# Weight blocks converted in pairs, one product with the reciprocal sums, and TensorE's fixed order from step 12, in a one-core attention and feed-forward kernel

## The chip, the cores and the metric

The kernel runs on one core of a Trainium2 chip. The metric is the device time of one execution in microseconds (us), as the median of several runs. A core has TensorE (PE, matmuls and transposes), VectorE (DVE), ScalarE (ACT), GpSimd (POOL) and SyncE (SP, which issues most transfers); each works through its own list of instructions in order, and semaphores make one wait for another.

## The reference

Attention with sink tokens and a sliding window, then a feed-forward block on its output:

```python
q, k, v: [4, 8, 768, 64] float32;  n_sink, window = 4, 128
w_in: [512, 2048], w_out: [2048, 512]   (float64)
scores = (q @ k.T) / 8
keep = (pos < n_sink) | ((0 <= rel) & (rel < window))
scores = where(keep, scores, -1e9); a = exp(scores - max)
a = a / (sum(a) + 1e-9);  x = (a @ v) as [3072, 512]
h = x @ w_in;  sp = max(h, 0) + log1p(exp(-|h|))
out = (h * erf(sp)) @ w_out
```

## The kernel before

The 3072 tokens form 12 groups of 256. Attention is cut into 48 steps, four head pairs for each group; step s is group s // 4. A step has these parts, written by one letter each in the order tables: q, v (loads), p (transposes of q and k into tile tqk, copied by ACT to kq), s (score matmuls into ps), f (`soft`: predicated copies and masking with the negative maximum on DVE, then four exponentials with their sums on ACT), n (`norm`: reciprocal of the sums and multiplication of the probabilities pst by it), t (transposes of pst into tile tp, copied by ACT to pt, masked by POOL into uo), w and u (the sink part: sh, ts, sp), a (value matmuls into av, two steps later), x (output of the step as the feed-forward's input, split into a high part xh and a low part xl). From step 9 on (NW) norm multiplies the sink columns apart (sh) and the four 128 x 128 parts of pst by four operations; before, the four parts are 128 x 144. In steps 4 to 7 the four are done on ACT.

Between the steps runs the feed-forward block, in 16 blocks of 128 hidden units per group: H m (hidden matmuls; two blocks share one tile h in one of two buffers), A m (the activation, seven operations on ACT and some on DVE, named r, u, acc, gf and g, with a product of three factors; its result g is split by POOL into two parts), P m (matmuls with w_out into tile o) and R (results). Group 0 works with the weights as single fp32 values (wf, gf, whole products of one matmul each), the others with weights split into a high part (h, `whigh`, a cast on ACT: wt from wf) and a low part (l, `wlow`, a subtraction on DVE), three matmuls for one.

The weights arrive as 64-bit words in 32 blocks of 512 KB (L j, `wload`, tile ws) and are turned into fp32 bits on DVE by three operations on 128 x 512 words each (C j, `wconv`, into half of a tile wf). `wconv` is a generator: one of its operations is put in after each operation of A or of norm (`fill`), and D drains what is left. All block tiles come from one pool of 33 buffers.

The order on each engine: the first steps follow three hand-written lists (LOADS for transfers, VEC for DVE, TEN for TensorE), where an item is placed once what it needs (`needs`) is placed. After these, every part has a key, `pos(s)` being the place of step s, and a scheduler takes ready instructions by priority. An engine's order is held to the keys only while `vec.on` or `ten.on` is set: DVE up to key 50, TensorE in the hand-written part and again from `pos(NF1) - 0.5` on (NF1 = 15). From step NI = 16 on, `together` does values, scores and transposes of a step as interleaved 64-row halves of the array, and q, k and pst of the neighbouring steps are flipped into one tile rt. The helper at L241 (`Line.run`) issues nearly every instruction of DVE and TensorE, so most rows of the trace carry its line.

Of the kernel before, what the change touches and what calls it, by code (L numbers as in the profile page):

```python
# [9 lines left out]
F32 = mybir.dt.float32  # L10
BF16 = mybir.dt.bfloat16
F32R = mybir.dt.float32r
I32 = mybir.dt.int32
AF = mybir.ActivationFunctionType
ALU = mybir.AluOpType
# [4 lines left out]
P = 128  # L20
# [14 lines left out]
LEAD, LAG = 16, 4  # L35

CEND = 50.0
WQ = 5
HI = 6.0
LO = 4.5  # L40

NE, AL = 4, 2
NW = 9
NF1 = 15
NI = 16

PW, EA = 256, 40
O = dict(prep=-100, norm=-100, core=-300, av=-300, load=-400, ptrans=-200, xfin=-100,
# [5 lines left out]
    "L18 L19 L20 L21 L22 q9 v9 L23 L24 L25 L26 L27 L28 L29 L30 L31"  # L54
)
VEC = (
# [3 lines left out]
)  # L60
TEN = (
    "p0 s0 p1 s1 p2 t0 u0 s2 t1 u1 p3 a0 x0 s3 a1 x1 t2 u2 p4 s4 a2 x2 t3 u3 p5 s5 a3 x3 t4 u4 H0 H1 H2 H3 p6 t5 u5 a4 s6 "
# [7 lines left out]
def kernel(  # L70
# [11 lines left out]
    nc = tc.nc  # L82
    B, H, S, D = q.shape
    NT, DM = out.shape
    DF = w_in.shape[1]
    NPAIR = H // 2
    NC = DM // P
# [6 lines left out]
    KB = P + SW  # L94
    scale = 1.0 / math.sqrt(D)

    cpool = ctx.enter_context(tc.tile_pool(name="const", bufs=1))
    wpool = ctx.enter_context(tc.tile_pool(name="wpool", bufs=33))


    ident = cpool.tile([P, P], F32, name="ident")
# [10 lines left out]
    wf = tiny[:, 4:8].rearrange("p (a b) -> p a b", a=2)  # L112
# [23 lines left out]
    wf, wt = {}, {}  # L136

    def fast_path():
        with ExitStack() as st:
# [4 lines left out]
            ps_o = st.enter_context(tc.tile_pool(name="ps_o", bufs=2, space=PSUM))  # L144
            ps_h = st.enter_context(tc.tile_pool(name="ps_h", bufs=2, space=PSUM))
            ps_s = st.enter_context(tc.tile_pool(name="ps_s", bufs=1, space=PSUM))
            first = ExitStack()
            ps_t = first.enter_context(tc.tile_pool(name="ps_t", bufs=2, space=PSUM))
            ps_r = []
# [10 lines left out]
                out=kw[:, :256], in0=rf[:, :256], scalar=0.0, in1=kw[:, :256], op0=ALU.is_ge, op1=ALU.mult  # L160
# [31 lines left out]
            pst = pers.tile([P, RING, 2, 2, KB], F32, name="pst")  # L192
# [55 lines left out]
            vec, ten, syn, sca = (Line(x) for x in (nc.vector, nc.tensor, nc.sync, nc.scalar))  # L248
# [10 lines left out]
            def prep(s):  # L259

                g, c = divmod(s, NPAIR)
                d = stp[s]
                if s <= NI:
                    tp = ps_t.tile([P, 4, P], F32, tag="t", name=f"tqk_{s}")
# [14 lines left out]
            def sinks(s):  # L279
# [14 lines left out]
            def score(s):  # L294
# [32 lines left out]

                if s >= NI:
                    together(s, half)
# [106 lines left out]
            def both(s):  # L436
                return shs[s % 2].rearrange("p r t -> p (r t)")[:, :P].bitcast(F32)

            def norm(s):
                d = stp[s]  # L440
                sm = d["sum"]
                vec.tensor_scalar_add(sm, sm, 1.0e-9)
                fill()
                vec.reciprocal(sm, sm)
                fill()
                if s >= NW:
                    x, y = (
                        t.rearrange("p (o n) t -> p o n t", o=1).broadcast_to([P, 2, 4, SW])
                        for t in (
                            d["pst"].rearrange("p i h t -> p (i h) t")[:, :, P:],  # L450
                            sm.rearrange("p i (h o) -> p (i h) o", o=1).broadcast_to([P, 4, SW]),
                        )
                    )
                    vec.tensor_tensor(both(s).rearrange("p (r n t) -> p r n t", r=2, n=4), x, y, op=ALU.mult)
                for i in range(2):
                    for h in range(2):
                        p = d["pst"][:, i, h, : P if s >= NW else KB]
                        if 4 <= s < 8:
                            nc.scalar.activation(p, p, AF.Copy, scale=sm[:, i, h : h + 1])
                        else:  # L460
                            vec.tensor_scalar_mul(p, p, sm[:, i, h : h + 1])

            def ptrans(s):

# [117 lines left out]
            staged, pair = {}, {}  # L582
            def wload(n):

                src = wblock(n)
                t = staged[n] = wpool.tile([P, 2 * DM], I32, tag="wo", name=f"ws_{n}")
                if src.dtype == F32:
                    syn.dma_start(t[:, :DM].bitcast(F32), src)
                else:
                    syn.dma_start(t, src.bitcast(I32))  # L590

            def wconv(n, wn):

                s = staged.pop(n)
                if wn // 2 not in pair:
                    pair[wn // 2] = wpool.tile([P, 2, DM], F32, tag="wo", name=f"wf_{wn // 2}")
                t = wf[n] = pair[wn // 2][:, wn % 2, :]
                if wblock(n).dtype == F32:
                    nc.scalar.copy(t, s[:, :512].bitcast(F32))
                    return  # L600
                w = s.rearrange("p (n t) -> p n t", t=2)
                ti = t.bitcast(I32)
                vec.tensor_scalar(ti, w[:, :, 1], 0x07FFFFFF, 3, op0=ALU.bitwise_and, op1=ALU.logical_shift_left)
                yield
                vec.scalar_tensor_tensor(
                    out=ti, in0=w[:, :, 1], scalar=-0x40000000, in1=ti, op0=ALU.bitwise_and, op1=ALU.bitwise_or
                )
                yield
                vec.scalar_tensor_tensor(
                    out=ti, in0=w[:, :, 0], scalar=29, in1=ti, op0=ALU.logical_shift_right, op1=ALU.bitwise_or  # L610
                )

            todo = []
# [12 lines left out]

            def whigh(n):

                d = wt[n] = wpool.tile([P, 2, DM], F32R, tag="wo", name=f"wt_{n}")
                nc.scalar.copy(d[:, 0, :], wf[n])  # L630

            def wlow(n):
# [4 lines left out]
            def wblock(n):  # L637
                if n < 16:
                    j, c = divmod(n, NC)
                    return w_in[c * P : (c + 1) * P, WB * j : WB * j + WB]  # L640
                return w_out[(n - 16) * P : (n - 15) * P, :]
# [29 lines left out]
            def use(n):  # L671
# [3 lines left out]
            order = sorted(range(32), key=use)  # L675
# [1 line left out]
                "q": ("load", loadqk), "v": ("load", loadv), "p": ("prep", prep), "k": ("prep", sinks), "s": ("core", score),  # L677
                "f": ("core", soft), "n": ("norm", norm), "t": ("ptrans", ptrans), "w": ("ptrans", sinkw), "u": ("ptrans", strans),
                "a": ("av", av), "x": ("xfin", xfin), "H": ("hid", hid), "A": ("act", act), "P": ("proj", proj), "R": ("res", res),
                "L": ("wl", lambda j: wload(order[j])), "C": ("wc", lambda j: todo.append(wconv(order[j], j))), "D": ("wc", drain),  # L680
                "h": ("ws", whigh), "l": ("ws", wlow),
            }

# [2 lines left out]

            def needs(nm, j):

                pin = [("C", order.index(n)) for n in range(j // NC * NC, j // NC * NC + NC)] if nm == "H" else []
                return {  # L690
                    "p": [("q", j), ("f", j - NPAIR)],
                    "s": [("p", j), ("f", j - 1 if j != 3 else 0)] if j > 1 else [("p", j)],
                    "f": [("s", j), ("t", j - (4 if j < 6 else 2)), ("w", j - (4 if j < 6 else 2))],
                    "n": [("f", j)],
                    "t": [("n", j), ("a", j - AL)],
                    "w": [("n", j), ("u", j - 2)] if j < NW else [("u", j)],
                    "u": [("w" if j < NW else "n", j), ("t", j)],
                    "k": [("v", j), ("p", j)],
                    "a": [("u", j), ("w", j), ("v", j)] + [("k", j)] * (j < NE),
                    "x": [("a", j)],  # L700
                    "H": pin + [("x", 3), ("f", 2), ("H", j - 1)] + [("A", j - 3)] * (j % 2 == 0),
                    "A": [("H", j), ("P", j - 4)],
                    "P": [("A", j | 1), ("C", order.index(16 + j if j < 16 else 0)), ("u", 5)],
                    "q": [("p", j - 2)],
                    "v": [("a", j - 3)],
                    "C": [("L", j)],
                    "L": [("C", j - WQ)],
                }.get(nm, [])

            lines = [words(x) for x in (LOADS, VEC, TEN)]  # L710
# [2 lines left out]
            while any(lines):  # L713
                before = len(done)
                for x in lines:
                    while x and all(w in done for w in needs(*x[0]) if w in known):
                        w = x.pop(0)
# [5 lines left out]

            fixed = pos(NF1) - 0.5
            for s in range(NE, NSTEP + AL):
                a = pos(s)
                if s < NF1:
                    plan = (
# [4 lines left out]
                else:  # L733
# [249 lines left out]
```

## Time and profile before

| | |
|---|---|
| median of 3 runs | 731.14 us (731.11 to 731.46) |
| profiled execution | 730.77 us, of which the span of the instructions is 729.1 us |
| TensorE busy | 695.0 us, 95% of the span |
| DVE busy | 517.6 us, 71% |
| ACT busy | 540.8 us, 74% |
| POOL busy | 193.4 us, 27% |
| mean granted TensorE clock | 0.994 of full speed |

The share of busy time is a mean over stages. A time line row gives the start, the busy time of a group of like instructions that follow each other, the engine, the line, the operation with its tiles (out<-in), and in brackets how long the engine stood idle before it and what it waited for. TensorE's matmuls overlap, so a group's busy time contains the tail of its last matmul, in which the next group already begins.

### The profile page before, as it was taken

The page shows a single profiled execution, that of the slowest core. Times are in us where ns is not written, and L with a number is a line of the kernel's source. Part 1 is how long each engine was busy: PE and PEld are TensorE (multiplying, and loading weights), DVE is VectorE, ACT ScalarE, POOL GpSimd, SP SyncE. Part 2 cuts the span into 40 slices and gives each one's busy share as a digit, 9 for nine tenths or more (in the row PEclk, how much of TensorE's full clock was granted, in tenths as well). Part 3 has the DMA queues.
Part 4 walks back from the last instruction along what each step waited for, and adds up shares of the span by engine and source line. Part 5 has one row for each costly group of instructions (what it writes and reads, how often), then busy time and mean ns, then how long its engine had stood idle before and what let it go on. Part 6 is the DMA issues. An engine that isn't in the chain of part 4 may idle for free. (4 is left out here: it accounts for less than half of the span.)

```text
span 729.1 us, 16134 instructions
## 1 busy us (share of the span) xinstructions
PE 695.0 (95%) x5721; PEld 588.3 (81%) x5721; DVE 517.6 (71%) x1493; ACT 540.8 (74%) x1288; POOL 193.4 (27%) x256
## 2 busy tenths in 40 slices
PE   4798999989999999999999999999999999999996
PEld 2474566777888888988888988988888988988995
DVE  7899998999786666666767667666767667663442
ACT  3576669778788778778878778778878778776663
POOL 2221010333232233234223223234223223232221
PEclk9999999999999999999999999999999999999999
DMA  5778641211212211112212212112212211100000
GB/s 142 213 208 307 212 142 27 63 27 37 60 36 53 59 38 44 55 29 47 58 37 52 59 34 49 55 27 46 59 34 57 58 31 38 41 1 1 30 1 33
DMA packets 100600, 47.40 MB, mean 65 GB/s; under 512 B 89248, under 2 KB 93344, under 8 KB 100512
## 3 DMA queue, kind: packets, MB, share of 16 engines
q1 hardware_dynamic: 99680, 46.16, 22.9%
q8 instruction: 47, 0.77, 0.4%
q14 instruction: 41, 0.34, 0.2%
q10 hardware_dynamic: 832, 0.13, 0.1%
HBM read 37.88 MB, written 6.29 MB: 61 GB/s over the span
## 5 line engine op out<-in xcount | busy, mean ns | idle before, releaser
L241 PE MATMUL o<-wt,g 128*128 128x512 f32 x1056 | 258.1, 393 | 1.1 <-POOLq L951 0.7
L241 PEld LDWEIGHTS o<-wt,g 128*128 128x128 f32 x1056 | 191.7, 188 | 39.3 <-POOLq L951 1.1
L810 POOL TENSOR_TENSOR g<-acc,g 128x512 fp32r<-128x512 f32 x88 | 116.8, 1327 | 382.5 <-DVE g L241 378.9
L241 PE MATMUL h<-xh,wt 128*128 128x256 f32 x1408 | 194.6, 281 | 2.2 <-DVE acc L241 2.1
L241 PEld LDWEIGHTS h<-xh,wt 128*128 128x128 f32 x1408 | 180.0, 189 | 9.0 <-DVE acc L241 3.2
L801 ACT ACTIVATE u<-r 128x512 f32<-128x512 f32 x288 | 162.1, 625 | 5.3 <-DVE gf L241 1.6
L241 DVE SCALAR_TENSOR_TENSOR acc<-u,h 128x512 f32<-128x512 f32 x88 | 60.5, 687 | 135.9 <-PE o L241 79.3
L241 DVE SCALAR_TENSOR_TENSOR acc<-u,acc 128x512 f32<-128x512 f32 x176 | 122.2, 694 | 18.0 <-ACT u L801 0.6
L241 PE MATMUL h<-xl,wt 128*128 128x256 f32 x704 | 110.0, 277 | 0.0
L796 ACT ACTIVATE r<-h 128x512 f32<-128x512 f32 x96 | 57.3, 596 | 68.4 <-PE h L241 68.3
L241 ACT ACTIVATE pst<-pst,kq 128x144 f32<-128x144 f32 x192 | 78.5, 421 | 22.7 <-DVE kq L241 22.4
L241 PEld LDWEIGHTS h<-xl,wt 128*128 128x128 f32 x704 | 93.4, 188 | 0.3 <-DVE wf L241 0.2
L487 POOL TENSOR_SCALAR_AFFINE_SELECT uo<-pt 128x512 f32<-128x512 f32 (+1 forms) x96 | 60.1, 649 | 89.9 <-ACT pt L241 89.8
L241 PE MATMUL ps<-kq 64*64 64x208 f32 (+1 forms) x768 | 70.3, 368 | 7.3 <-ACT kq L241 7.3
L241 PE MATMUL av<-uo,v 64*64 64x192 f32 (+4 forms) x856 | 70.0, 294 | 0.0
L797 ACT ACTIVATE r<-r 128x512 f32<-128x512 f32 x96 | 60.9, 635 | 2.7
L798 ACT ACTIVATE r<-r 128x512 f32<-128x512 f32 x96 | 60.9, 634 | 2.8
L241 PEld LDWEIGHTS ps<-kq 64*64 64x64 f32 x768 | 41.5, 138 | 20.7 <-issue 9.7
L241 PEld LDWEIGHTS av<-uo,v 64*64 64x64 f32 (+1 forms) x856 | 47.7, 134 | 10.3 <-issue 1.9
L241 ACT COPY kq<-rt 128x512 f32<-128x512 f32 (+1 forms) x39 | 19.1, 511 | 46.0 <-PE rt L241 46.0
L241 DVE CUSTOM_DVE_ANT_0 pst<-ps,mask 128x144 f32<-128x144 f32 x192 | 47.6, 304 | 1.6
L241 DVE CAST g<-acc 128x512 fp32r<-128x512 f32 x88 | 38.2, 434 | 8.4
(98 smaller groups left out, 713.7 us busy)
## 6 DMA issues: line engine op xcount, KB each, us to landing
ws<-in_moe_w_in_dram SPq DMA_DIRECT2D x16, 512.0 KB, 5.0
ws<-in_moe_w_out_dram SPq DMA_DIRECT2D x16, 512.0 KB, 7.7
v<-in_v_dram SPq DMA_DIRECT2D x64, 96.0 KB, 2.3
out_dram<-ot SPq DMA_DIRECT2D x24, 256.0 KB, 2.2
q<-in_q_dram SPq DMA_DIRECT2D x95, 64.0 KB, 2.4
k<-in_k_dram SPq DMA_DIRECT2D x95, 64.0 KB, 2.3
v<-in_v_dram SPq DMA_DIRECT2D x32, 64.0 KB, 2.3
kq<-kq SPq DMA_DIRECT2D x32, 64.0 KB, 1.8
```

Of the source, the lines that this page charges most:

```text
L241: ins = f(*a, **k)
L487: nc.gpsimd.affine_select(out=uo[:, :, i1:, e, :], in_=pt[:, :, i1:, :], pattern=[[0, 2], [0, 2 - i1], [-sg, P]], compare_op=op, fill=0.0, ...
L796: nc.scalar.activation(r, h, AF.Tanh, bias=b_t, scale=0.5)
L797: nc.scalar.activation(r, r, AF.Square, bias=b_v, scale=-0.5)
L798: nc.scalar.activation(r, r, AF.Square, bias=b_r)
L801: nc.scalar.activation(u, r, AF.Square, bias=b_a[i], scale=CS)
L810: nc.gpsimd.tensor_tensor(gl, acc, gh.bitcast(F32), op=ALU.subtract)
```

## The change

Conversion: blocks 0 to 3 are converted singly as before, the other 28 in 14 pairs, three DVE operations over 128 x 1024 words each. The raw words lie in a pool of their own (`wraw`, three tiles of two blocks), the other blocks' pool has 27 buffers in place of 33, and a load waits for the conversion that used its tile before. Where the raw pool lay, a pool `wlate` of six buffers opens once it is closed; the split weights with places 20 to 25 in the order of use (blocks 12 to 15 of w_in, 24 and 25 in the count over both matrices) go there. The list VEC names a pair by its even member. Norm: outside steps 4 to 7 the four products of pst become one TENSOR_TENSOR with the reciprocal sums broadcast. Order: NF1 is 12 and NI is 13, so TensorE is held to the keys from step 12 on and works in halves from step 13 on; keys of t, u and P that depend on them change too.

```diff
-WQ = 5
+SOLO = 4
...
-NF1 = 15
-NI = 16
+NF1 = 12
+NI = 13
...
-    "D f6 x4 C12 A3 n6 C13 D w6 C14 C15 A5 C16 C17 D f7 x5 C18 C20 A7 n7 C19 C21 D w7 C22 C23 A9 C24 C25 D f8 x6 C26 A11 n8 "
-    "C27 D w8 C28 C29 A13 x7 C30 C31 D f9 A15"
+    "D f6 x4 C12 A3 n6 D w6 C14 A5 C16 D f7 x5 C18 A7 n7 C20 D w7 C22 A9 C24 D f8 x6 C26 A11 n8 "
+    "D w8 C28 A13 x7 C30 D f9 A15"
...
-    wpool = ctx.enter_context(tc.tile_pool(name="wpool", bufs=33))
+    wpool = ctx.enter_context(tc.tile_pool(name="wpool", bufs=27))
...
+            early = ExitStack()
+            wraw = [early.enter_context(tc.tile_pool(name="wraw", bufs=3, side="right"))]
+            late = []
...
-                for i in range(2):
-                    for h in range(2):
-                        p = d["pst"][:, i, h, : P if s >= NW else KB]
-                        if 4 <= s < 8:
+                n = P if s >= NW else KB
+                if 4 <= s < 8:
+                    for i in range(2):
+                        for h in range(2):
+                            p = d["pst"][:, i, h, :n]
                             nc.scalar.activation(p, p, AF.Copy, scale=sm[:, i, h : h + 1])
-                        else:
-                            vec.tensor_scalar_mul(p, p, sm[:, i, h : h + 1])
+                    return
+                p = d["pst"].rearrange("p i h t -> p (i h) t")[:, :, :n]
+                x = sm.rearrange("p i (h o) -> p (i h) o", o=1).broadcast_to([P, 4, n])
+                vec.tensor_tensor(p, p, x, op=ALU.mult)
...
-                t = staged[n] = wpool.tile([P, 2 * DM], I32, tag="wo", name=f"ws_{n}")
+                j = order.index(n)
+                if j // 2 not in staged:
+                    staged[j // 2] = wraw[0].tile([P, 2, 2 * DM], I32, tag="w", name=f"ws_{j // 2}")
+                t = staged[j // 2][:, j % 2, :]
...
+                n = 1 if j < SOLO else 2
+                s = staged[j // 2][:, j % 2 : j % 2 + n, :]
...
+                t = pair[j // 2][:, j % 2 : j % 2 + n, :]
...
-                d = wt[n] = wpool.tile([P, 2, DM], F32R, tag="wo", name=f"wt_{n}")
+                if 20 <= order.index(n) < 26:
+                    if not late:
+                        early.close()
+                        late.append(st.enter_context(tc.tile_pool(name="wlate", bufs=6, side="right")))
+                    d = wt[n] = late[0].tile([P, 2, DM], F32R, tag="wo", name=f"wt_{n}")
+                else:
+                    d = wt[n] = wpool.tile([P, 2, DM], F32R, tag="wo", name=f"wt_{n}")
...
-                    "C": [("L", j)],
-                    "L": [("C", j - WQ)],
+                    "C": [("L", j if j < SOLO else j + 1)],
+                    "L": [("C", z) for z in (whole(j - j % 2 - 6), whole(j - j % 2 - 5)) if z[1] >= 0],
```

TensorE's own instructions around step 12, before: h_28 are the last hidden matmuls ahead of it, o are the matmuls with w_out (wt_24 and wt_25 are its blocks), tp_12 and ts_12 the transposes of step 12, h_30 the next hidden matmuls.

```order
L241 MATMUL h_28_1859<-xl_1_723,wt_15_1550 128x256
L241 MATMUL o_1_0_1484<-wt_24_1552,g_25_1735 128x512
...
L241 MATMUL o_1_1_1485<-wt_25_1612,g_25_1735 128x512
L241 MATMUL tp_12_1875<-ident_61,pst_138 128x128
L241 MATMUL ts_12_1884<-ident_61,sh0_139 128x128
L241 MATMUL tp_12_1875<-ident_61,pst_138 128x128 x3
L241 MATMUL h_30_1936<-xh_1_722,wt_12_1544 128x256 x2
```

The same place in the change (its helper is at L246), with av_11 and ps_13 as the first values and scores in halves, rt_13 the first joint tile of flips.

```order
L246 MATMUL h_28_1791<-xl_1_711,wt_15_1488 128x256
L246 MATMUL tp_12_1822<-ident_61,pst_145 128x128 x4
L246 MATMUL ts_12_1831<-ident_61,sh0_146 128x128
L246 MATMUL o_1_0_1418<-wt_24_1490,g_25_1670 128x512
...
L246 MATMUL o_1_1_1419<-wt_25_1544,g_25_1670 128x512
L246 MATMUL av_11_1869<-sp_11_1618,sv_143 128x256
...
L246 MATMUL rt_13_1896<-ident_61,q_14_1711 128x64 x4
L246 MATMUL h_30_1926<-xh_1_710,wt_12_1482 128x256 x2
```

The transposes of step 12 have moved from behind the twelve o matmuls to ahead of them, and values, scores and flips of step 13 from behind h_30 to ahead of it.

ACT's instructions ahead of the exponentials of step 9 (pst_138 with its four parts), before: wt are the casts of `whigh`, kq_134 is the copy of step 10's transposes, r and u belong to the activations.

```order
L801 ACTIVATE u2_15_1244<-r_15_1233 128x512
L241 COPY kq_134<-tqk_10_1209 128x4x128
L630 CAST wt_21_1402<-wf_8_862 128x512
L630 CAST wt_22_1465<-wf_9_917 128x512
L241 ACTIVATE pst_138,kq_134<-pst_138,kq_134 128x144 x4
L796 ACTIVATE r_17_1310<-h_16_1280 128x512
```

The same place in the change; wt_12 is the first tile in `wlate`, and pst_145 is the tile that was pst_138.

```order
L826 ACTIVATE u2_15_1171<-r_15_1160 128x512
L652 CAST wt_12_1482<-wf_10_883 128x512
L652 CAST wt_13_1484<-wf_10_883 128x512
L652 CAST wt_14_1486<-wf_11_987 128x512
L652 CAST wt_15_1488<-wf_11_987 128x512
L652 CAST wt_24_1490<-wf_12_997 128x512
L246 COPY kq_141<-tqk_10_1178 128x4x128
L652 CAST wt_25_1544<-wf_12_997 128x512
L246 ACTIVATE pst_145,kq_141<-pst_145,kq_141 128x144 x3
L821 ACTIVATE r_17_1241<-h_16_1211 128x512
L246 ACTIVATE pst_145,kq_141<-pst_145,kq_141 128x144
```

The six casts of the late pool stand ahead of these exponentials now, where two others stood, and the first operation of r_17 stands between the third and the fourth. At step 12 the first operation of r_27 has come between the third and the fourth exponential in the same way:

```order
L246 COPY kq_141<-tqk_13_1704 128x3x16
L821 ACTIVATE r_27_1773<-h_26_1717 128x512
L246 ACTIVATE pst_145,kq_141<-pst_145,kq_141 128x144 x3
L822 ACTIVATE r_27_1773<-r_27_1773 128x512
L246 ACTIVATE pst_145,kq_141<-pst_145,kq_141 128x144
```

Before, the four of step 12 stood together, behind all of r_27 and its u, and ahead of r_29.

## Rows read from the trace of the kernel before

**Rows 1.** Windows: stretch, its length, busy time of each engine, PEclk, DMA, GB/s.

```profile
0.00:153.35 153.35, 128.06 (x770) 87.48 (x771) 138.88 (x404) 104.68 (x270) 28.33 (x58) 0.98 0.53 158
150.00:180.00 30.00, 26.51 (x197) 21.04 (x196) 27.78 (x69) 23.57 (x58) 10.10 (x13) 1.00 0.10 24
210.00:720.00 510.00, 509.93 (x4538) 454.02 (x4536) 329.60 (x961) 389.25 (x904) 144.40 (x174) 1.00 0.15 39
```

**Rows 2.** Time line of TensorE at step 12 and at step 15.

```profile
163.67 1.20 PE L241 MATMUL h<-xh,wt 128*128 128x256 f32 x8 [0.33 <-DVE acc L241]
...
166.52 1.08 PE L241 MATMUL o<-wt,g 128*128 128x512 f32 x4
167.89 2.11 PE L241 MATMUL o<-wt,g 128*128 128x512 f32 x8 [0.30 <-POOL g L810]
170.80 0.30 PE L241 MATMUL tp<-ident,pst 128*128 128x128 f32 x1 [0.80 <-ACT wt L630]
...
172.34 1.21 PE L241 MATMUL h<-xh,wt 128*128 128x256 f32 x8 [0.64 <-DVE acc L241]
...
197.81 0.30 PE L241 MATMUL tp<-ident,pst 128*128 128x128 f32 x1 [0.22 <-DVE pst L241]
```

**Rows 3.** Time line of DVE at norm 12.

```profile
169.75 0.17 DVE L241 TENSOR_SCALAR kq<-kq 128x4 f32<-128x4 f32 x1 [0.16 <-ACT pst L241]
...
170.38 0.87 DVE L241 TENSOR_SCALAR pst<-pst,kq 128x128 f32<-128x128 f32 x4
...
177.05 0.69 DVE L241 SCALAR_TENSOR_TENSOR acc<-u,h 128x512 f32<-128x512 f32 x1
```

**Rows 4.** Time line of ACT, the operation behind step 12's exponentials.

```profile
169.63 0.57 ACT L796 ACTIVATE r<-h 128x512 f32<-128x512 f32 x1
```

**Rows 5.** Time lines of DVE and ACT from the last conversion to norm 9.

```profile
114.15 2.50 DVE L241 SCALAR_TENSOR_TENSOR wf<-ws,wf 128x512 int32<-128x512 int32 x4
...
120.72 0.16 DVE L241 TENSOR_SCALAR kq<-kq 128x4 f32<-128x4 f32 x1
...
116.83 0.56 ACT L241 COPY kq<-tqk 128x512 f32<-128x512 f32 x1
117.29 1.14 ACT L630 CAST wt<-wf 128x512 fp32r<-128x512 f32 x2
118.33 0.42 ACT L241 ACTIVATE pst<-pst,kq 128x144 f32<-128x144 f32 x1
...
119.95 0.58 ACT L796 ACTIVATE r<-h 128x512 f32<-128x512 f32 x1
```

**Rows 6.** DVE by shape (count, busy, mean ns, idle before), then two of its time line.

```profile
L241 DVE SCALAR_TENSOR_TENSOR wf<-ws,wf 128x512 int32<-128x512 int32 x64 | 43.0, 712 | 0.4
L241 DVE TENSOR_TENSOR xl<-av,xh 128x256 fp32r<-128x256 f32 x44 | 18.5, 420 | 0.1
...
65.15 1.42 DVE L241 SCALAR_TENSOR_TENSOR wf<-ws,wf 128x512 int32<-128x512 int32 x2
122.12 3.09 DVE L241 TENSOR_TENSOR wt<-wf,wt 128x512 fp32r<-128x512 f32 x5
```

**Rows 7.** Time line of TensorE behind three idle times, and a window.

```profile
29.20 0.99 PE L241 MATMUL ps<-kq 64*64 64x208 f32 x16 [1.73 <-ACT kq L241]
37.21 1.60 PE L241 MATMUL ps<-kq 64*64 64x208 f32 x16 [3.04 <-ACT kq L241]
61.83 1.99 PE L241 MATMUL h<-xf,wf 128*128 128x256 f32 x8 [2.09 <-DVE gf L241]
...
37.46:40.84 3.38, 3.38 (x26) 1.70 (x19) 2.93 (x13) 1.45 (x6) 0.47 (x1) 0.50 0.59 163
```

**Rows 8.** Windows: an old step's flips of pst, its rest, a whole step in halves.

```profile
186.08:186.54 0.46, 0.46 (x7) 0.46 (x6) 0.46 (x1) 0.04 (x1) 0.00 (x0) 1.00 0.00 0
189.95:192.29 2.34, 2.34 (x31) 1.38 (x29) 1.99 (x4) 2.31 (x6) 0.67 (x2) 1.00 0.06 13
228.40:230.80 2.40, 2.40 (x51) 1.87 (x50) 1.99 (x3) 1.16 (x3) 0.02 (x1) 1.00 0.00 0
```

More of the change, by code (lines that the diff above doesn't have):

```diff
@@ L146, in fast_path @@
             ps_s = st.enter_context(tc.tile_pool(name="ps_s", bufs=1, space=PSUM))
+            edge = st.enter_context(tc.tile_pool(name="edge", bufs=1, side="right"))
+            edge.tile([P, 24], F32, name="edge")
+            early = ExitStack()
+            wraw = [early.enter_context(tc.tile_pool(name="wraw", bufs=3, side="right"))]
+            late = []
             first = ExitStack()
@@ L590, in wload, with wconv @@
                     syn.dma_start(t, src.bitcast(I32))
[L592 to L599, printed above, removed]
+            def wconv(j):
+                n = 1 if j < SOLO else 2
+                s = staged[j // 2][:, j % 2 : j % 2 + n, :]
+                if (j + n) % 2 == 0:
+                    staged.pop(j // 2)
+                if j // 2 not in pair:
+                    pair[j // 2] = wpool.tile([P, 2, DM], F32, tag="wo", name=f"wf_{j // 2}")
+                t = pair[j // 2][:, j % 2 : j % 2 + n, :]
+                for i in range(n):
+                    wf[order[j + i]] = t[:, i, :]
+                if wblock(0).dtype == F32:
+                    nc.scalar.copy(t, s[:, :, :512].bitcast(F32))
                     return
-                w = s.rearrange("p (n t) -> p n t", t=2)
+                w = s.rearrange("p m (n t) -> p m n t", t=2)
                 ti = t.bitcast(I32)
-                vec.tensor_scalar(ti, w[:, :, 1], 0x07FFFFFF, 3, op0=ALU.bitwise_and, op1=ALU.logical_shift_left)
+                vec.tensor_scalar(ti, w[:, :, :, 1], 0x07FFFFFF, 3, op0=ALU.bitwise_and, op1=ALU.logical_shift_left)
                 yield
                 vec.scalar_tensor_tensor(
-                    out=ti, in0=w[:, :, 1], scalar=-0x40000000, in1=ti, op0=ALU.bitwise_and, op1=ALU.bitwise_or
+                    out=ti, in0=w[:, :, :, 1], scalar=-0x40000000, in1=ti, op0=ALU.bitwise_and, op1=ALU.bitwise_or
                 )
@@ L609, in wconv @@
                 vec.scalar_tensor_tensor(
-                    out=ti, in0=w[:, :, 0], scalar=29, in1=ti, op0=ALU.logical_shift_right, op1=ALU.bitwise_or
+                    out=ti, in0=w[:, :, :, 0], scalar=29, in1=ti, op0=ALU.logical_shift_right, op1=ALU.bitwise_or
                 )
@@ L679, in fast_path @@
                 "a": ("av", av), "x": ("xfin", xfin), "H": ("hid", hid), "A": ("act", act), "P": ("proj", proj), "R": ("res", res),
-                "L": ("wl", lambda j: wload(order[j])), "C": ("wc", lambda j: todo.append(wconv(order[j], j))), "D": ("wc", drain),
+                "L": ("wl", lambda j: wload(order[j])), "C": ("wc", lambda j: todo.append(wconv(j))), "D": ("wc", drain),
                 "h": ("ws", whigh), "l": ("ws", wlow),
@@ L687, in needs, with whole @@
             def needs(nm, j):
-                pin = [("C", order.index(n)) for n in range(j // NC * NC, j // NC * NC + NC)] if nm == "H" else []
+                def whole(n):
+                    return ("C", n if n < SOLO else n - n % 2)
+                pin = [whole(order.index(n)) for n in range(j // NC * NC, j // NC * NC + NC)] if nm == "H" else []
                 return {
@@ L702, in needs @@
                     "A": [("H", j), ("P", j - 4)],
-                    "P": [("A", j | 1), ("C", order.index(16 + j if j < 16 else 0)), ("u", 5)],
+                    "P": [("A", j | 1), whole(order.index(16 + j if j < 16 else 0)), ("u", 5)],
                     "q": [("p", j - 2)],
                     "v": [("a", j - 3)],
-                    "C": [("L", j)],
-                    "L": [("C", j - WQ)],
+                    "C": [("L", j if j < SOLO else j + 1)],
+                    "L": [("C", z) for z in (whole(j - j % 2 - 6), whole(j - j % 2 - 5)) if z[1] >= 0],
                 }.get(nm, [])
```

2 rows, old and new, of the table VEC are left out of this document.

## The prediction

> **What bounds the kernel now.** I read the windows first, engine by engine. Up to 153.35 us TensorE works 128.06 of 153.35 us while VectorE (DVE) is busy for 138.88; from 150 to 180 us it is 26.51 against 27.78 of 30; from 210 to 720 us TensorE works 509.93 of 510.00 [rows 1]. So there are two stages. Early, DVE paces and TensorE waits for it; later TensorE has a backlog that never empties, and the end comes when it is worked off. Whatever TensorE loses or saves before the backlog begins moves the end one for one; a microsecond saved on DVE counts only as far as TensorE starts something earlier by it.
>
> Then TensorE's time line at step 12, the last loop before the backlog. It shows waits of 0.33, 0.30 and 0.80 us, and after the transposes of step 12 (tp_12, 170.80) the hidden matmuls h_30 start at 172.34 [rows 2]. The waits are for DVE, whose norm of step 12 runs from 169.75 to 171.25 [rows 3]; that norm follows the last exponential, which ScalarE (ACT) has done when r_29 starts at 169.63 [rows 4]. This loop, 162 to 179 us, is where the change decides itself, since from step 16 on the order of TensorE is the one it had.
>
> I write S for the lead of DVE in the changed kernel over DVE before, in us, at the start of step 12's hidden matmuls h_28. TensorE enters the loop by DVE's products (h_28 waits for acc), so both move by S together.
>
> **Part one: TensorE's order.** In the old order h_28 starts at 163.67 and is followed at 166.52 by the twelve matmuls o of blocks 24 and 25, which fill most of the time until tp_12's data are there. In the new order tp_12 and ts_12 stand ahead of these twelve. TensorE is done with h_28 at 166.6 − S, and then nothing behind tp_12 can start.
>
> When do its data come? The new ACT order has one operation (r_27, 0.57 us by the like of r_29 [rows 4]) between the third and fourth exponential, so the last ends at 170.20 − S instead of 169.63. DVE's first small operation follows 0.12 later, as before (169.75 after 169.63), and the product 0.63 after that (170.38 after 169.75) [rows 3]: 170.95 − S. The four old products took 0.87 in all, and the first transpose could go 0.42 after the first product began (170.80 after 170.38), 0.14 after its end, taking a quarter as 0.28. Now the transposes wait for the whole product, which I price at 0.68 (below): 171.63, plus 0.14, gives 171.77 − S. With 0.46 for the transposes [rows 8] TensorE is through at 172.2 − S. It was through, and began h_30, at 172.34. It has stood still some 5.2 us and still has the twelve o before it: in two pieces they took 3.19 there with the drain of each [rows 2], some 2.8 in one piece. At this point it is 172.2 + 2.8 − 172.34 = **2.7 us behind, less S**.
>
> **Part two: halves from step 13.** An old step costs TensorE 2.34 (values, scores, next transposes) and 0.46 (probabilities), together 2.80; the halves do it all in 2.40 [rows 8]. Steps 14 and 15 gain 0.40 each. Step 13 has no probabilities to flip in halves (step 12 is flipped in the old way) and step 16 had halves before but for tp_15; I give these two 0.2 each as an estimate. Sum 1.2. It comes back at any time after 172, since TensorE is backlogged. Bounds: 0.8 (two steps) to 1.6 (four). The new order before step 12 also swaps work on TensorE, at nothing: DVE is late there, not TensorE.
>
> **Part three: does anything wait after tp_12?** h_30 takes the hidden buffer of h_28 now (av_13's tile takes h_26's), so it waits for the first product acc_29. That began at 177.05 and lasted 0.69 [rows 3]; DVE comes out of norm 12 some 0.4 later than before (171.63 against 171.25), so it ends at about 178.15 − S. TensorE arrives at 172.2 + 2.8 + 2.35 (step 13 in halves) = 177.35 − S: a wait of **0.8**, unless TensorE is slower until then.
>
> It may be. Idle TensorE was followed by its lower level here: after an idle 3.04 us the scores of a step took 1.60 instead of 0.99, and from 37.46 to 40.84 us the granted clock was 0.50 [rows 7], the 1.2 of its two levels, 1.2 and 2.4 GHz. After the idle 2.09 before 61.83 the profile shows no fall that I can see: eight hidden matmuls took 1.99. The stall that I expect, 5.2 us, is longer than either, so I take a fall. By the row it lasts 3.38 us and costs half of that, **1.7**, and it covers the wait of 0.8. Bounds 0.8 (full clock) to 1.7. The Trainium skill, "TensorE: Matmul & The Clock Gate", Part 1, says that the throttled state is the default and that activity releases it; by that rule alone the fall is due and the sum would be the one with 1.7, which the trace bears out at 37 us, and not at 62.
>
> **Part four: how large S is.** Conversions. Four blocks are converted as before. Of the 14 pairs I count 7 that are drained in one go and 7 whose operations alternate with others. An operation over 512 columns is issued every 0.60 (five in 3.09: four starts 0.60 apart and the last one's 0.68), though a conversion's operation lasts 0.71 by its mean; one over 256 columns takes 0.42 where one over 512 takes 0.68 [rows 6], so 512 more columns cost 0.52, one operation of 1024 columns 1.12 where two took 1.20. Three such operations save 0.24 where others stand between; where each waits for the one before it, I give nothing, since two interleaved blocks hid that. 7 × 0.24 = 1.7. The merged product: 0.68 for 512 columns, or 0.60 by the pitch, against 0.87 for four; it saves 0.17 on DVE in each of the five norms 0 to 3 and 8, 0.85. Bounds per product: it loses 0.25 (1.12, should it run like one of double width) or saves 0.27 (0.60). Lost: in norm 6, ACT multiplies, and the conversion of block 13 (two operations of 1.42 together [rows 6] and a third) ran under it; as a pair it is done before, and DVE idles there: −1.4. Sum at the end of the last conversion: **S0 = +1.1**. Bounds 0 (pairs save nothing) to 3 (all 14 pairs gain, norm 6 loses nothing).
>
> Then a new gate. Six converted blocks (12 to 15, 24, 25) now get their high parts in memory that the raw words occupied, so the first cast, wt_12, waits for the end of DVE's last conversion, at 116.65 (114.15 + 2.50) [rows 5]. Behind it on ACT, in its order, stand five casts, the copy kq_10, and only then the exponentials of step 9. Two casts took 1.04 to the next start, the copy 0.46 (116.83 to 117.29), the exponentials 1.62 (118.33 to 119.95) [rows 5], and r_17 now stands among them (0.6). The last exponential ends at 116.65 − S0 + 0.1 + 3.1 + 0.5 + 1.6 + 0.6 = 122.55 − S0, and norm 9 starts 0.1 later; before it started at 120.72 [rows 5]. So DVE's lead becomes S0 − 1.9, and norms 9 to 11 give 0.5 back: S = S0 − 1.4, or −0.3, between −1.4 and +1.6. I take the middle of the bounds, **S = 0**. Weight loads now wait for conversions three pairs back; the trace of before has no such wait, so the bounds are nothing and one pair's operations (six of 0.6 to 0.7 before, about 3 us); I take nothing, as DVE works 138.88 of the first 153.35 us [rows 1] and so mostly finds its blocks landed.
>
> **Sum.** 2.7 − 1.2 + 1.7 − 0 = +3.2 us against the profiled execution's 730.77, that is 733.9; the median of the runs shown lies 0.37 higher, so 734.3. I round to **734.2**. What the measurement can tell from no change is about 0.2%, 1.46 us either way (729.7 to 732.6).
>
> **The rivals.** *The clock holds* (chance 0.18): the stall is there, only the wait of 0.8 is added: 2.7 − 1.2 + 0.8 = +2.3, 733.4. For it speaks the row at 61.83; against it the one at 37.21.
> *DVE's gains arrive whole* (0.17): the gate on wt_12 costs nothing, because ACT has slack there, and S is 2 to 3. Then the sum is +0.2 to +1.2 with a fall, −0.7 to +0.3 without one: 730.4 to 732.3, mostly the same. Against it: all six casts stand ahead of exponentials for which DVE waits.
> *Faster* (0.12): the same place, with DVE early enough. The old order had tp_15 at such a place too, and it cost TensorE only 0.22 (197.81 [rows 2]). TensorE's loss is 2.7 − 1.2 + 0.8 = 2.3 at S = 0; from S = 2.3 on there is none, and from 3.8 on the kernel is faster by more than 0.2%; at S = 4.5 it takes 728.9. TensorE has 25 us of idle time before 153 us [rows 1], so there is room for it. Against it: S0 reaches 3 only if every part of it pays.
> *The ring starves* (0.06): a load that waits for a conversion three pairs back lands late, and DVE stops for about 3 us: 737.
> The forecast keeps 0.47, with its own range of 732.6 to 735.7 (S from −1.4 to +1.6).
>
> **Numbers.** Slower: 0.46 of the forecast, 0.15 of the held clock, 0.03 of the gains and 0.06 of the ring, 0.70. Same: 0.01, 0.03 and 0.12 of the first three, 0.16. Faster: the 0.12 and 0.02 of the gains, 0.14. The range leaves out the starving ring and most of the faster case: 730.3 to 736.2.
>
> **What would show it.** In the changed profile: TensorE idle for some 5 us ahead of tp_12, released by DVE's product, with a granted clock of 0.50 for some 3 us behind it; wt_12 waiting for a conversion on ACT, and norm 9 later, or not earlier, relative to the last conversion; merged products of about 0.68; steps 14 and 15 in 2.40 on TensorE. The prediction is wrong if the idle time before tp_12 is under 3 us, if DVE's lead at h_28 is over 2 us, or if TensorE shows new idle time after 180 us.

## The result and the profile after

The changed kernel takes **737.06 us** (median of 6, 736.26 to 738.17) against 731.14 for the kernel before (6 runs): ratio 1.0082, 95% interval 1.0072 to 1.0092, some 5.9 us slower. Slower was forecast; 734.2 us was too little, and 737.06 lies above the range of 730.3 to 736.2. The profiled execution (736.26, the shortest of the six) has a span of 734.5 us, 5.4 more than before.

The windows of the changed kernel, cut where the transposes of step 11 begin (tp_11; at 153.35 us before, at 154.77 now), answer to [rows 1]; three short ones behind them follow what happened next.

```profile
0.00:154.77 154.77, 124.49 (x771) 86.12 (x771) 134.96 (x340) 104.20 (x270) 30.20 (x58) 0.99 0.53 156
154.77:734.50 579.73, 567.42 (x5003) 502.87 (x5003) 371.73 (x980) 434.30 (x1015) 166.32 (x202) 0.99 0.16 40
...
156.50:160.23 3.73, 3.73 (x29) 2.01 (x29) 3.63 (x4) 1.89 (x4) 3.60 (x4) 0.58 0.09 20
160.23:163.05 2.82, 0.00 (x2) 0.01 (x1) 2.76 (x7) 1.81 (x4) 0.00 (x0) 0.94 0.20 49
163.05:167.90 4.85, 4.85 (x28) 4.85 (x29) 4.44 (x8) 1.22 (x4) 1.26 (x1) 0.65 0.26 57
```

TensorE comes to tp_11 1.42 us later than before. From there on the span before has 575.75 us with 566.95 of TensorE busy, the one after 579.73 with 567.42: 3.98 us longer, of them 3.5 idle and 0.5 busy. The busy part hides two things that nearly cancel. The granted clock was 0.58 and 0.65 in two stretches, so TensorE lost 0.42 × 3.73 + 0.35 × 4.85 = 3.3 us there; without them its work would be 2.8 less than before, for which I hold the halves and the undivided groups of matmuls to be the reason.

TensorE's time line of the changed kernel at step 12 answers to [rows 2].

```profile
154.77 0.30 PE L246 MATMUL tp<-ident,pst 128*128 128x128 f32 x1 [1.19 <-DVE pst L246]
...
156.50 0.38 PE L246 MATMUL av<-sp,sv 128*128 128x256 f32 x1 [1.00 <-ACT pt L246]
156.81 1.72 PE L246 MATMUL av<-uo,v 128*64 128x128 f32 x12
158.46 1.77 PE L246 MATMUL ps<-kq 64*64 64x208 f32 x16
163.05 0.44 PE L246 MATMUL tqk<-ident,k 128*128 128x128 f32 x2 [2.82 <-DVE sp L246]
...
163.46 1.66 PE L246 MATMUL h<-xh,wt 128*128 128x256 f32 x8
...
173.45 0.60 PE L246 MATMUL tp<-ident,pst 128*128 128x128 f32 x4
...
173.91 3.00 PE L246 MATMUL o<-wt,g 128*128 128x512 f32 x12
...
200.66 1.18 PE L246 MATMUL h<-xh,wt 128*128 128x256 f32 x8 [1.56 <-DVE sp L246]
```

There is no bracket at tp_12 (173.45), where I had put 5.2 us. TensorE stood still earlier: 1.00 us ahead of the values of step 10 (av_10) and 2.82 ahead of tqk_13. These two stand in the fixed order ahead of the hidden matmuls h_26; before, h_26 (154.88) came first, and tqk_13 (162.75) came behind the matmuls o of blocks 22 and 23 (159.88), as four rows of the kernel before show:

```profile
154.88 1.20 PE L241 MATMUL h<-xh,wt 128*128 128x256 f32 x8 [0.64 <-DVE acc L241]
...
157.74 0.28 PE L241 MATMUL av<-sp,sv 128*128 128x256 f32 x1
...
159.88 3.03 PE L241 MATMUL o<-wt,g 128*128 128x512 f32 x12
162.75 0.38 PE L241 MATMUL tqk<-ident,k 128*128 128x128 f32 x2
```

In the change av_10 takes the tile of tp_11, which ACT's copy pt_11 frees at 156.45, and tqk_13 takes that of ts_11, which DVE's sp_11 frees. Two rows of DVE show the latter, and where DVE stands; the third is acc_25 in the kernel before:

```profile
162.42 0.57 DVE L246 TENSOR_TENSOR sp<-ts,sp 32x128 fp32r<-32x128 f32 x2
...
163.75 0.69 DVE L246 SCALAR_TENSOR_TENSOR acc<-u,h 128x512 f32<-128x512 f32 x1
...
162.93 0.69 DVE L241 SCALAR_TENSOR_TENSOR acc<-u,h 128x512 f32<-128x512 f32 x1
```

sp_11 ends at 162.99 and tqk_13 starts at 163.05. DVE itself is 0.8 us later than before, S = −0.8.

DVE and ACT at the last conversion and norm 9, which answer to [rows 5], and DVE by shape, which answers to [rows 6].

```profile
113.24 2.50 DVE L246 SCALAR_TENSOR_TENSOR wf<-ws,wf 128x1024 int32<-128x1024 int32 x2
...
121.86 0.17 DVE L246 TENSOR_SCALAR kq<-kq 128x4 f32<-128x4 f32 x1 [1.97 <-ACT pst L246]
...
116.06 2.68 ACT L652 CAST wt<-wf 128x512 fp32r<-128x512 f32 x5
118.65 0.57 ACT L246 COPY kq<-tqk 128x512 f32<-128x512 f32 x1
119.12 0.62 ACT L652 CAST wt<-wf 128x512 fp32r<-128x512 f32 x1
119.64 0.41 ACT L246 ACTIVATE pst<-pst,kq 128x144 f32<-128x144 f32 x1
...
121.33 0.41 ACT L246 ACTIVATE pst<-pst,kq 128x144 f32<-128x144 f32 x1
...
L246 DVE SCALAR_TENSOR_TENSOR wf<-ws,wf 128x1024 int32<-128x1024 int32 x28 | 35.5, 1268 | 0.4
L246 DVE TENSOR_TENSOR pst<-pst,kq 128x512 f32<-128x512 f32 x39 | 26.7, 684 | 0.0
```

The last conversion ends at 115.74, 0.9 us earlier than before (116.65). The six casts and the copy follow, the last exponential starts at 121.33, and DVE stands 1.97 us idle for it: norm 9 is 1.1 us later than before. The lead of 0.9 has become a lag. ACT does not stand idle for the conversion: the row of the casts at 116.06 has no bracket. What makes the norm late is that 3.1 us of casts stand ahead of the exponentials.

### The profile page after: what moved, and what is told of

The parts are those of the page before. It is cut to its first block, busy times and chain, and to the rows that moved or that the text cites. A ratio compares the mean times of both kernels' runs of the same rounds, so it can differ in the third digit from the quotient of the medians.

```text
span 734.5 us, 16062 instructions
## 1 busy us (share of the span) xinstructions
PE 691.9 (94%) x5773; PEld 589.0 (80%) x5773; DVE 506.7 (69%) x1319; ACT 538.5 (73%) x1284; POOL 196.5 (27%) x260
## 5 line engine op out<-in xcount | busy, mean ns | idle before, releaser
L246 PE MATMUL o<-wt,g 128*128 128x512 f32 x1056 | 257.0, 392 | 1.2 <-POOLq L976 0.7
L246 PEld LDWEIGHTS o<-wt,g 128*128 128x128 f32 x1056 | 191.9, 188 | 38.6 <-POOLq L976 1.1
L246 PE MATMUL h<-xh,wt 128*128 128x256 f32 x1408 | 195.8, 282 | 2.0 <-DVE sp L246 1.6
L246 PEld LDWEIGHTS h<-xh,wt 128*128 128x128 f32 x1408 | 181.4, 191 | 7.3 <-ACT r L823 2.0
L246 DVE SCALAR_TENSOR_TENSOR acc<-u,h 128x512 f32<-128x512 f32 x88 | 60.5, 687 | 140.3 <-PE o L246 82.4
L246 DVE SCALAR_TENSOR_TENSOR acc<-u,acc 128x512 f32<-128x512 f32 x176 | 121.8, 692 | 19.1 <-ACT u L826 1.2
L246 PE MATMUL h<-xl,wt 128*128 128x256 f32 x704 | 109.5, 277 | 0.0
L246 PEld LDWEIGHTS h<-xl,wt 128*128 128x128 f32 x704 | 93.6, 189 | 0.0
L246 ACT ACTIVATE pst<-pst,kq 128x144 f32<-128x144 f32 x192 | 78.0, 418 | 19.6 <-DVE kq L246 19.3
L246 PE MATMUL ps<-kq 64*64 64x208 f32 (+1 forms) x768 | 72.6, 371 | 8.5 <-ACT kq L246 8.5
L246 PE MATMUL av<-uo,v 64*64 64x192 f32 (+4 forms) x884 | 71.9, 292 | 0.0
L246 PEld LDWEIGHTS ps<-kq 64*64 64x64 f32 x768 | 42.8, 139 | 22.3 <-ACT kq L246 10.5
L246 PEld LDWEIGHTS av<-uo,v 64*64 64x64 f32 (+1 forms) x884 | 49.4, 134 | 10.3 <-issue 1.7
L246 ACT COPY kq<-rt 128x512 f32<-128x512 f32 (+1 forms) x44 | 21.0, 501 | 48.9 <-PE rt L246 48.2
L246 DVE CUSTOM_DVE_ANT_0 pst<-ps,mask 128x144 f32<-128x144 f32 x192 | 47.6, 304 | 1.6
L246 DVE CAST g<-acc 128x512 fp32r<-128x512 f32 x88 | 38.5, 438 | 8.6
```

Source lines behind the costliest of these rows:

```text
L246: ins = f(*a, **k)
```

## The experiments

Two theories were put against each other. A: most of the loss is TensorE's fixed order of step 12, with the clock behind its waits. B: it is late DVE work, by the conversions, the casts and the product. Each result is the ratio to the kernel before on the same chip in the same hours, with its 95% interval; 1% is 7.3 us. The medians of before moved between 731.0 and 732.9 from one group of runs to the next, so an expected time is to be read as its distance from 731.1 (or, where it says so, from another version).

**Conversions, late pool and product alone.**

```diff
-NF1 = 12
-NI = 13
+NF1 = 15
+NI = 16
```

> The changed kernel with NF1 = 15 and NI = 16 put back: paired conversions, late pool and merged product alone. Theory A (TensorE's fixed order makes most of the loss: idle 1.00 and 2.82 us ahead of the scores' and the next transposes' place, the clock behind it, 1.56 at 200.66): only DVE's lateness of some 1.0 us stays, 731.5 to 732.5. Theory B (late DVE work makes it): most of the 5.9 us stays, 735 to 737.

Measured 1.0012 (1.0004 to 1.0021), 733.52 against 732.94: 0.9 us by the ratio. As theory A had it.

**The order alone**, in the kernel before.

```diff
-NF1 = 15
-NI = 16
+NF1 = 12
+NI = 13
```

> The kernel before with NF1 = 12 and NI = 13 alone. Theory A: idle time 2.8 us more than before, 2.4 for the clock, 1.2 gained by the halves, +4.0: 735.1 (734 to 736.5). Theory B: no more than +1, under 732.2.

Measured 1.0058 (1.0045 to 1.0071), 736.89 against 732.94, 4.0 to 4.3 us. Theory A again; 0.9 and 4.3 make 5.2 of the 5.9, and the rest is within the three intervals.

**The fixed order without early halves**: NF1 = 12 alone in the kernel before.

> The kernel before with NF1 = 12 alone (halves still from step 16): the fixed order of step 12 without early halves. If the order makes most of the loss: the idle time of 2.8 to 3.3 us at 162 and the clock behind it stay, 2.5 to 4.5 us above the kernel before. If the early halves make it: under 1.5 us above.

Measured 1.0051 (1.0037 to 1.0064), 734.64 against 730.98, 3.7 us. Its profiled execution (736.46, the longest of five) shows both waits of the changed kernel on TensorE, with old conversions and old products:

```profile
156.03 0.39 PE L241 MATMUL av<-sp,sv 128*128 128x256 f32 x1 [1.25 <-ACT pt L241]
...
162.80 0.44 PE L241 MATMUL tqk<-ident,k 128*128 128x128 f32 x2 [2.82 <-DVE sp L241]
```

So the fixed order from step 12 on costs nearly all that the order change costs, and the early halves on top of it bring nothing that can be told: 1.0058 with, 1.0051 without. With them TensorE waits 1.43 us at 199.57, and the version without them has no such wait.

**tqk_13 where it was**, the rest as in the change.

```diff
-("p", a - (4.28 if s > NF1 else 2.87), s),
+("p", a - (4.28 if s > NF1 + 1 else 2.87), s),
```

> The changed kernel with the transposes of q and k of step 13 (tqk_13) at the key they had, behind the matmuls o of blocks 22 and 23. If the stall only moves on (my forecast's place): the 2.82 us go, TensorE then stands some 3 to 5 us ahead of the transposes of step 12, 736 to 737.5. If the place alone was at fault: 2.8 us less idle time and some of the clock's 2.4, 732 to 734.

Measured 1.0051 (1.0038 to 1.0064), 736.69 against 732.94: 3.7 us above before, where the change is 5.9 above on its chip. Its TensorE, time line and two windows:

```profile
156.06 0.38 PE L246 MATMUL av<-sp,sv 128*128 128x256 f32 x1 [1.00 <-ACT pt L246]
156.37 1.09 PE L246 MATMUL av<-uo,v 128*64 128x128 f32 x12
...
171.28 0.69 PE L246 MATMUL tp<-ident,pst 128*128 128x128 f32 x4 [3.95 <-DVE pst L246]
171.76 0.42 PE L246 MATMUL ts<-ident,sh 128*128 128x128 f32 x1
171.83 4.53 PE L246 MATMUL o<-wt,g 128*128 128x512 f32 x12
...
156.06:159.79 3.73, 3.73 (x41) 2.92 (x42) 3.63 (x4) 1.82 (x4) 3.63 (x4) 1.00 0.19 46
171.28:176.19 4.91, 4.91 (x17) 4.02 (x18) 4.71 (x7) 3.35 (x8) 3.39 (x4) 0.65 0.00 0
```

The wait moved on to the place of my forecast: 3.95 us ahead of tp_12, released by DVE's product, with the clock at 0.65 behind it (0.35 × 4.91 = 1.7 us, the price that I had). In the change the first wait had used this one up. So the wait was where the first expectation had it; the time, 3.7 us above before, lies between the two (5 to 6 and 1 to 3 above). In the traces TensorE waits more here, not less (1.00 and 3.95, against 1.00 and 2.82 in the change), but its clock falls once and not twice: behind the same 1.00 at av_10, with 1.17 at tp_11 before it, it stayed at 1.00 here (156.06 to 159.79). That stretch stands in the same order in both versions, so how much of the gain is the edit's and how much the clock's is not shown.

**The casts behind step 9's copy**, the rest as in the change.

```diff
+ins = nc.scalar.copy(d[:, 0, :], wf[n])
+if 20 <= order.index(n) < 26:
+    follow(tail["pt", 9], ins)
```

> The changed kernel with the six casts into the late pool held behind the copy of step 9's transposes on ACT. If the gate makes DVE late: norm 9 starts some 2 us earlier against the end of the conversions, DVE leads by 0.8 to 1 at step 12 and the time falls by 1 to 2, 735 to 736. If ACT had the slack anyway: within 0.5 of 737.1.

Measured 1.0050 (1.0037 to 1.0063), 735.66 against 732.94: 2.7 to 3.7 us above before, some 2 to 3 below the change, where 1 to 2 were expected. DVE leads by 2.7 us at acc_25 (160.23, before 162.93), but TensorE gains less, because the fixed order makes it wait longer for the same sp_11:

```profile
159.53 0.69 PE L246 MATMUL tqk<-ident,k 128*128 128x128 f32 x2 [4.23 <-DVE sp L246]
...
160.23 0.69 DVE L246 SCALAR_TENSOR_TENSOR acc<-u,h 128x512 f32<-128x512 f32 x1
```

**NF1 = 13 with NI = 13**, the rest as in the change: everything of step 12 in its old place, halves from step 13.

> The changed kernel with NF1 = 13 (NI stays 13): TensorE is held to the keys from step 13 on, so tqk_13, the transposes of step 12 and the matmuls o of blocks 24 and 25 stand as before, and halves still begin at step 13. If the fixed order of step 12 makes the loss: no idle time over 1 us at 163, DVE's lateness of 0.9 us and the 1.6 us wait near 200 stay, the halves give back 1.2: some 1.3 us above the kernel before (0.5 to 2). If the halves themselves at steps 13 to 16 make it: 3 to 5 us above.

Measured 1.0043 (1.0030 to 1.0056), 736.33 against 732.93, 3.2 us. The waits near 163 are gone, and two others stand in TensorE's time line:

```profile
176.12 0.34 PE L246 MATMUL rt<-ident,k 64*128 64x64 f32 x4 [1.51 <-issue]
...
177.87 2.01 PE L246 MATMUL h<-xh,wt 128*128 128x256 f32 x8 [1.29 <-DVE acc L246]
...
177.87:182.33 4.46, 4.46 (x25) 4.46 (x25) 4.10 (x10) 0.74 (x3) 2.82 (x3) 0.62 0.30 65
```

The tile rt_13 opens in the memory of the old transposes' tiles and starts 0.1 us after DVE's sp_12 (175.44 + 0.58), so I take sp_12 to release it, though the profile says "issue"; h_30 waits for acc_29, since its hidden buffer was h_28's, which is the kind of wait of the prediction's part three (0.8 there, 1.29 here). The clock falls once more. That is at the upper of the two expectations, by waits for the halves' own tiles.

**NF1 = 13 without early halves**, in the kernel before.

> The kernel before with NF1 = 13 alone (halves still from step 16). The stall at rt_13, 1.5 us, and that of h_30, 1.3, which the one with NF1 = 13 and NI = 13 showed, come from the halves' tiles: so here neither should be, and the time is within 1 us of the kernel before. If they come from the keys of step 13: 2 to 3 us above.

Measured 1.0022 (1.0014 to 1.0031), 732.66 against 730.98, 1.6 us. Neither the rt wait nor that of h_30 is there, but the order from step 13 on costs two waits of the kind of step 12, the second smaller. The time is in between the two expectations:

```profile
172.94 0.38 PE L241 MATMUL av<-sp,sv 128*128 128x256 f32 x1 [1.25 <-ACT pt L241]
...
176.00 0.44 PE L241 MATMUL tqk<-ident,k 128*128 128x128 f32 x2 [0.75 <-DVE sp L241]
```

**The sink copies on ACT**: in the version with NF1 = 13, those of steps 14 to 16 on ACT instead of POOL.

```diff
-(nc.gpsimd.tensor_copy if s < NE or s > NI else nc.scalar.copy)
+(nc.gpsimd.tensor_copy if s < NE or s > 16 else nc.scalar.copy)
```

> As the one with NF1 = 13, and the copies of the sink values of steps 14 to 16 stay on ACT, as before, in place of POOL. If DVE's and with it TensorE's wait near 200 us comes from these copies on POOL: that wait goes and the time falls by 1 to 1.6 us. If they wait for the load of v whoever copies them: no difference, within 0.4.

Measured 1.0069 (1.0056 to 1.0082), 737.43 against 732.93: 1 to 2 us slower than with the copies on POOL, where neither expectation had a loss; what causes it is open. The wait near 200 is still there, 1.69 for 0.88 with the copies on POOL, and the copy waits for the load of v on ACT too (ACT, then TensorE):

```profile
197.32 0.62 ACT L290 CAST sv<-v 32x128 fp32r<-32x128 f32 x2 [2.56 <-DMA v<-in_v_dram]
...
200.20 1.06 PE L246 MATMUL h<-xh,wt 128*128 128x256 f32 x7 [1.69 <-DVE sp L246]
```

**And the casts moved in it.**

> As the last, and the six casts into the late pool stand behind step 9's copy on ACT. DVE should lead by 2 to 2.7 us at step 12, as it did with the casts moved alone; without the fixed order of step 12 TensorE can use it: 1.5 to 2.5 us below the one without, 1.5 to 3 us below the kernel before. If DVE's lead is lost again at step 12: within 0.5 of the one without.

Measured 1.0038 (1.0025 to 1.0051), 735.67 against 732.93, 1.8 below the one without but not below the kernel before. Five executions lie between 735.5 and 735.8 and one at 731.4; that one was profiled, and its clock never fell (mean 1.000, against 0.990 to 0.995 of the other five). Its TensorE:

```profile
173.08 0.34 PE L246 MATMUL rt<-ident,k 64*128 64x64 f32 x4 [1.51 <-issue]
...
174.83 1.18 PE L246 MATMUL h<-xh,wt 128*128 128x256 f32 x8 [1.28 <-DVE acc L246]
...
174.83:179.29 4.46, 4.46 (x32) 4.17 (x33) 4.10 (x12) 2.68 (x8) 1.68 (x1) 1.00 0.29 65
```

It has the waits of the version with NF1 = 13 and NI = 13 (1.51 and 1.29), behind which the clock fell to 0.62 there; here it stayed at 1.00. No trace of the other five exists, so that the clock makes these 4 us is argued, not shown.

**The first part with the casts moved**: the order of before (NF1 = 15, NI = 16).

> Paired conversions, late pool and merged product with the order of before (NF1 = 15, NI = 16), and the six casts behind step 9's copy. If the gate on these casts was the reason why this part cost 0.9 us: it gains now, 1 to 2 us below the kernel before. If the merged product or the pairs cost it: still 0.5 to 1 us above.

Measured 0.9984 (0.9975 to 0.9993), 731.54 against 732.93. From 1.0012 to 0.9984, each against the kernel before on its own chip, by the place of six casts alone: their place costs 0.28%, 2 us, and it was the reason why this part lost. DVE in this version: the last conversion ends at 115.05, norm 9 starts at 119.12 with no idle time.

```profile
112.55 2.50 DVE L246 SCALAR_TENSOR_TENSOR wf<-ws,wf 128x1024 int32<-128x1024 int32 x2
...
119.12 0.16 DVE L246 TENSOR_SCALAR kq<-kq 128x4 f32<-128x4 f32 x1
```

**The merged product alone**, in the kernel before.

> The kernel before with the merged product alone. By my price DVE gains 0.17 us in a norm, but the first transpose waits for the whole product: nothing, within 0.6 us. If the wait for the whole product is what counts (0.4 us in each step that TensorE waits for): 0.6 to 1.5 us above.

Measured 1.0003 (0.9994 to 1.0012): nothing, as priced. In its trace TensorE waits 1.19 us ahead of the transposes of step 12 and 0.20 ahead of h_30, where before it was 0.80 and 0.64 [rows 2]; h_30 starts 0.95 us earlier than before (171.39), and a wait of 1.60 ahead of the transposes of step 15, for 0.22 before, takes that back.

**Pairs and moved casts with four products**, the order of before.

> The order of before with paired conversions, the late pool and the six casts behind step 9's copy, but four products in each norm. If the merged product costs TensorE its wait of 0.4 us in steps 8 to 12: 0.4 to 1 us under the one that has it too, 1.5 to 2.5 us below the kernel before. If it pays: above that one.

Measured 0.9986 (0.9977 to 0.9994), 729.88 against 730.98, 1.0 us faster than before, and not to be told from the one with the merged product: the price of the product is nothing here too.

**Halves from step 15, and from step 14**, in this last version (NF1 = NI = 15, and 14).

> The version with pairs, moved casts and four products, with NF1 = 15 and NI = 15: halves one step earlier than before. If halves pay as soon as TensorE has its backlog: 0.3 to 0.6 us under the one with NI = 16. If their tiles still wait for DVE at step 15: 1 us or more above it.

> The same with NF1 = 14 and NI = 14, two steps earlier. If the switch loses while DVE still paces, as it did at 13: 1 to 3 us above the one with NI = 16, with waits at the first tile rt and at the hidden matmuls behind it. If the loss at 13 was something of that step alone: 0.6 to 1 us under it.

Measured 1.0018 (1.0009 to 1.0027) and 1.0006 (0.9997 to 1.0015), where NI = 16 gave 0.9986. Both lose, by some 2.3 and 1.5 us. TensorE's brackets, the first from 15, the others from 14:

```profile
205.03 1.21 PE L246 MATMUL h<-xh,wt 128*128 128x256 f32 x7 [1.89 <-DVE acc L246]
...
188.23 0.34 PE L246 MATMUL rt<-ident,k 64*128 64x64 f32 x4 [0.38 <-ACT r L821]
190.27 1.21 PE L246 MATMUL h<-xh,wt 128*128 128x256 f32 x8 [1.58 <-DVE acc L246]
```

The halves take one of the two hidden buffers for their values, so the hidden matmuls behind them wait for DVE's product with the other. I take it that up to step 16 TensorE is not far enough behind DVE to hide that.

## Why the prediction was wrong

**The step that failed** is the sentence of part two that "the new order before step 12 also swaps work on TensorE, at nothing: DVE is late there, not TensorE". It is just where DVE is late that TensorE's order costs: putting av_10 and tqk_13, which wait for DVE and ACT, ahead of h_26 and of o of blocks 22 and 23, which were ready (with tqk_13 put back they start without a wait), made TensorE idle for 1.00 and 2.82 us, and its clock fell behind both waits in the profiled execution. I let TensorE enter h_28 at its old time less S; it came to it 7 us later (170.71 against 163.67), with tqk_13, h_26 and the o matmuls rearranged before it. At tp_12 I had it 2.7 us behind; measured, it was through with tp_12 at about 173.9 and not 172.2, so 4.4 behind. In the two versions with this order and the old conversions, where S is nothing, it was through at 173.1 and 173.7.

Of the 2.7 us by which the sum fell short (3.2 for 5.9), the order has 0.8 to 1.1 (4.0 to 4.3 alone, for 3.2), and S, which I took as 0, has 0.9 (the conversions, late pool and product alone); the rest is within the intervals. Two of the prediction's own signs of being wrong came: no idle time ahead of tp_12, and new idle time after 180 us.

**Part one's mechanism** was right in kind and wrong in place. The stall that I put ahead of tp_12 was a real one (3.95 us where tqk_13 is put back), but the earlier one hid it. The piece of TensorE's order that is shown with the change begins with h_28; one that began at tp_11 would have shown tqk_13 ahead of h_26. A reading was loose too: of the three waits before step 12 that I gave to DVE, the profile puts 0.30 down to POOL's g, and 0.80 to ACT [rows 2], though for the latter DVE's product fits [rows 3].

**Part two's size**: the work of TensorE from tp_11 on is 2.8 us less where I had 1.2 for steps 13 to 16, though that sum also holds drains between split groups. Counted from the end of tp_12 and without its twelve o, it is 1.4 less (549.26 for 550.67), and step 14 took the 2.40 that I had (190.96 to 193.36): the halves' work was priced rightly. But from tp_12 to the end the change lost another 1.0 where I had a gain of 1.2 and a fall of the clock of 1.7, so +0.5: TensorE's idle time there grew by 2.4 (8.5 for 6.1), and 1.56 of it, the wait at 200.66, was not foreseen. It comes from a load of v: an operation of DVE that needs its copy stands ahead of most of the masking of the scores, and DVE stands idle 1.87 us for it. The wait is in the version with the order alone (1.43) and not in that without early halves. Early halves brought nothing in any version.

**Part three**: the clock was priced rightly for one fall (1.7 us in the version with tqk_13 put back) and fell twice in the change, 3.3. The wait of h_30 was there in the versions with NF1 = 13 and NI = 13, which had no stall at tp_12 of the forecast's size (1.29, for 0.8); with tqk_13 put back, where the stall and the fall came as I had them, h_30 did not wait. The Trainium skill, "TensorE: Matmul & The Clock Gate", Part 1, calls the throttled state the default, which activity releases. The trace agrees at 156.50, where the clock was 0.58 behind idle times of 1.19 and 1.00 us, but not at 61.83 of [rows 7], nor with tqk_13 put back, where idle times of 1.17 and 1.00 left it at 1.00.

**Part four**: S0 was 0.9 for 1.1. The gate took 2.0 for 1.9 (norm 9 1.1 later than before, from a lead of 0.9), by the casts' place in ACT's list and not by a wait, and moving them gave back 2 us. Two bounds of S0 do not follow from their terms (all 14 pairs with the products give 4.2 and not 3, no gain from the pairs −0.6 and not 0), which did not matter. S was −0.8, where my working had −0.3 and I took 0. The pairs' operations that alternate with others came 1.14 apart where I had 1.12, the product lasted 0.68 as priced. No load came late: the 28 wide conversions had 0.4 us of idle time ahead of them in all. So the starving ring was not the cause, though its price, 737, came nearest to the measured time, by luck: six operations of 0.6 to 0.7 us are 3.6 to 4.2, not 3.

**The rivals.** The clock did not hold, DVE's gains did not arrive whole, and the faster case needed a lead of DVE that only the moved casts gave; with the order of the change even that version stayed 2.7 to 3.7 us above the kernel before.

## What to carry to other kernels

In these runs, fixing the list of an in-order engine was safe where that engine was the one that is behind. Fixed earlier, the same order put instructions that wait for the slower engine ahead of others that were ready, and in the change each fall of TensorE's clock behind such a wait added 1.6 to 1.7 us. Before an order is priced, write down for each instruction moved forward what it waits for and what stands behind it, beginning with the first one moved and not with the one that the change is about. And when memory is given to work that comes later, see where its first users end up in their engine's list, since everything behind them comes later as well: six casts ahead of the exponentials cost 2 us more than the same six behind one copy.

## What was not expected of the hardware

A wait of 1.00 us behind one of 1.19 was followed by a granted clock of 0.58 over the next 3.7 us, though single waits of 1.93 us (at 62 us) and 1.75 (at 104) earlier in the same execution had left it at 1.00. In the version with NF1 = 13 two waits close together, 1.51 and 1.29, were followed by 0.62. But two waits close together do not settle it: 1.17 and 1.00 (tqk_13 put back), 1.20 and 0.99 (casts moved) and 1.51 and 1.28 (NF1 = 13 with copies and casts moved) left the clock at 1.00. So did 0.78 and 1.25 (NF1 = 13 without early halves), where 0.79 and 1.25 (NF1 = 12 without early halves) were followed by 0.55 over 3.8 us. The five waits of 2.82 to 4.23 us ahead of tqk_13 or tp_12 were each followed by a fall, to between 0.59 and 0.70. One execution of each version was traced, so whether one program falls at such a pair in some executions and not in others was not tried.
